# Attention beside two matrix layers on one core: its transfers moved to SyncE's queue, a second k and v buffer, and ScalarE and VectorE in the order of emission through layer 1

## The chip, the cores and the metric

One core of a Trainium2 chip runs the whole program. The time is device microseconds of one execution on that core; the kernel before was run three times. The engines are TensorE (PE, with its weight loads as PEld), VectorE (DVE), ScalarE (ACT), GpSimd (POOL) and SyncE (SP); SP only issues transfers here. Transfers that GpSimd issues show in the profile as queue q0 (software_dynamic), those that SP issues as q1 (hardware_dynamic).

## What is computed

Attention without a softmax, its normalized output laid out as 4608 rows of 512, then two layers without biases. Inputs are float32: q, k, v of 8 batches x 8 heads x 576 positions x 64, and for each layer w_in (512 x 2048) and w_out (2048 x 512).

```python
kv  = np.einsum('bhsd,bhse->bhde', k, v)
out = np.einsum('bhsd,bhde->bhse', q, kv)
x   = out / np.sqrt(np.mean(out * out, axis=-1, keepdims=True) + 1e-06) * g_norm
# x: batch, head, position, 64  ->  4608 x 512
h = x @ w_in;  g = h * (1.0 / (1.0 + np.exp(-1.702 * h)));  x = g @ w_out    # layer 1
h = x @ w_in2; g = h - np.tanh(h);                          y = g @ w_out2   # layer 2
```

## The kernel before, in words

**Stages.** The loop at the end of `body` runs `l` over the two layers and `n` over eight blocks of 576 tokens; block n of layer 1 is batch n of the attention. "Stage n" in this document is stage n of layer 1 (l = 0) unless layer 2 is named. Each stage has two halves. In m1 the block is multiplied by w_in, in m2 by w_out. Every operand is split into two float16 parts, and a product takes three matmuls (lines 631 to 633 in m1, 817 to 819 in m2; lines 845 to 847 and 888 to 890 in the plain forms of stages 0 and 1). From stage 2 on, m1 is a scheme of seven products in place of eight: 54 steps of six matmuls and two more that are run between the first steps of m2. ScalarE copies a bank (L664) and applies the activation (L638), VectorE adds two products (L669). m2 has 28 steps of twelve matmuls; VectorE prepares operands (L692), ScalarE and VectorE split them (L706, L712), five steps ahead of TensorE, and ScalarE and VectorE finish results (L760, L754). The w_out weights of m2 come as 14 streams of 512 KB (`stream`, L733, SP), each for two steps, into four buffers; the first four of a stage are asked for after m1 is emitted, the others when a buffer has been used.

**Work beside the stages.** Three kinds of side work are Python generators that are advanced at the end of every step by `tick`, at a rate per step that the main loop gives (first rate m1, second m2). One advance up to the next `yield` is a "call" in this document.

- `front(b)` computes attention's first part for batch b on TensorE: k-transposed-v products (`head_products`, L425) of units (kt, i), copied by ScalarE (L426), the numerators (`pair_numerators`, L434), their squares and scaled copies on ScalarE (L467, L468), the mean squares (`pair_squares`, L441, read by L443 and L445) and the roots (L507, L508, with two table loads).
- `back(b)` refines the roots on VectorE (`newton`, L513, L514), stores them to `rd` in HBM, loads them back spread over the partitions (L564), multiplies (L571), and splits the result into the float16 operand `xo` of the next stage (`xprep`, L336 on VectorE, L346 on ScalarE, L349 on VectorE).
- `conv1` converts layer 2's weights, 32 items. It loads raw words of item k+1 (`load_words`, L144 and L145, GpSimd), starts item k with ScalarE's L156, goes on with VectorE (L159 to L174), ScalarE's L224 and VectorE's L177, and stores the item (L229 or L232, GpSimd). One item is seven calls; two raw buffers alternate, and the stored item lies in its raw buffer, so the load of item k+1 waits for the store of item k-1. It runs from stage 2's m2 on, from stage 3 at 0.62 and 0.5 calls per step.

In stage n from 2 on, `back(n + 1)` runs beside m1 and, up to stage 5, `front(n + 2)` beside m2. Stage 0 has front(1) and back(1), stage 1 has front(2), back(2) and front(3).

**Transfers of attention.** `part` (L378 to L381) asks for a piece of the packed q, k, v (`atp`), from GpSimd's queue: 1280 words per partition for a unit of k and v (640 KB), 1152 for the q of a pair (576 KB). One region `rk` holds one unit of k and v, so a unit is asked for when the one before has been used; `rq` holds a q, `rs` and `rx` hold results.

**Order.** The tile framework places the instructions of an engine by its own timeline, save inside `tc.manual_schedule`, where the named engines keep the order in which the program emits them. Until the end of stage 1 these are PE, SP, DVE and ACT; from stage 2 on they are PE and SP alone (line 1110). Side instructions get an edge after the latest main instruction of their engine (`issue_after`), so they may come later than emitted, not earlier.

```python
            s[2] += s[1][m]
            while s[2] >= 1:
                s[2] -= 1
```

## Time and profile before

| what | value |
|---|---|
| median of 3 runs | 1529.11 us (1528.98 to 1531.12) |
| profiled execution | 1537.64 us, span 1535.7 us |
| busy share of the span | PE 94%, VectorE 76%, ScalarE 58%, GpSimd 10% |
| layer 1, stages 0 to 7 | 35 to 867 us of the span |
| layer 2 | 867 to 1536 us |
| chain that ended last | PE 45%, DVE 19%, issue 19%, DMA 11%, ACT 5% |

Matmuls overlap in their records, so a busy TensorE is not one at its peak: 288 columns show as some 0.29 us each and start 0.12 us after one another. The rows below give, for a stretch, each engine's busy time with its instructions in brackets, then TensorE's granted clock (1.00 is 2.4 GHz, 0.50 is 1.2 GHz), the DMA engines' busy share and GB/s. A half of a stage is a stretch between the first m1 matmul and the first m2 matmul of a block, or back.

### The profile page before, as it was taken

The page shows a single profiled execution, that of the slowest core. Times are in us where ns is not written, and L with a number is a line of the kernel's source. Part 1 is how long each engine was busy: PE and PEld are TensorE (multiplying, and loading weights), DVE is VectorE, ACT ScalarE, POOL GpSimd, SP SyncE. Part 2 cuts the span into 40 slices and gives each one's busy share as a digit, 9 for nine tenths or more (in the row PEclk, how much of TensorE's full clock was granted, in tenths as well). Part 3 has the DMA queues.
Part 4 walks back from the last instruction along what each step waited for, and adds up shares of the span by engine and source line. Part 5 has one row for each costly group of instructions (what it writes and reads, how often), then busy time and mean ns, then how long its engine had stood idle before and what let it go on. Part 6 is the DMA issues. An engine that isn't in the chain of part 4 may idle for free.

```text
span 1535.7 us, 29954 instructions
## 1 busy us (share of the span) xinstructions
PE 1441.6 (94%) x11922; PEld 1112.7 (72%) x11922; DVE 1159.7 (76%) x2237; ACT 892.7 (58%) x1871; POOL 152.5 (10%) x238
## 2 busy tenths in 40 slices
PE   6999978998899889998999999999999999999999
PEld 5667756676666666766777777777777777777777
DVE  3998878394885976967978686887778787868585
ACT  5775554664765756747656564645565555656463
POOL 0001010102322222111110000000000000000000
PEclk9999999999999999999999999999999999999999
DMA  8776836437477387384586516061523334240504
GB/s 285 220 239 192 249 92 203 129 115 249 125 238 226 90 269 225 124 287 131 178 292 228 181 34 222 14 203 39 171 85 132 124 104 136 71 154 31 194 15 155
DMA packets 104684, 247.55 MB, mean 161 GB/s; under 512 B 10624, under 2 KB 55296, under 8 KB 104544
## 3 DMA queue, kind: packets, MB, share of 16 engines
q1 hardware_dynamic: 83504, 161.49, 32.6%
q0 software_dynamic: 21040, 84.15, 17.4%
q8 instruction: 93, 1.52, 0.4%
q14 instruction: 47, 0.39, 0.1%
HBM read 202.62 MB, written 42.98 MB: 160 GB/s over the span
## 4 chain that ended last, share of the span: by engine, by line
PE 45%; DVE 19%; issue 19%; DMA 11%; ACT 5%; POOL 1%; SPq 0%; DVEq 0%; ACTq 0%; POOLq 0%
PE X L817 4%; PE X L818 4%; PE X L819 4%; PE X L631 3%; PE X L632 3%; PE X L633 3%; DVE gt L692 3%; DVE jt L712 3%; DMA scratch<-rd 2%; PE Y L817 2%; PE Y L819 2%; PE Y L818 2%; PE Z L631 2%; PE Z L633 2%; PE Z L632 2%
## 5 line engine op out<-in xcount | busy, mean ns | idle before, releaser
L706 ACT ACTIVATE jt<-gt 128x576 f16<-128x576 f32 x420 | 284.5, 682 | 179.7 <-PE X L819 73.6
L712 DVE SCALAR_TENSOR_TENSOR jt<-gt,jt 128x576 f16<-128x576 f32 x420 | 312.9, 753 | 95.9 <-ACT jt L706 92.8
L817 PE MATMUL X<-jt,st 128*128 128x288 f16 x960 | 278.6, 290 | 16.8 <-ACT mscratch L760 14.8
L818 PE MATMUL X<-jt,st 128*128 128x288 f16 x960 | 278.4, 290 | 3.7 <-DVE jt L712 3.7
L819 PE MATMUL X<-jt,st 128*128 128x288 f16 x960 | 278.1, 290 | 0.0
L631 PE MATMUL X<-xo,wi 128*128 128x288 f16 x896 | 256.8, 287 | 19.5 <-ACT mscratch L664 17.8
L632 PE MATMUL X<-xo,wi 128*128 128x288 f16 x896 | 256.8, 287 | 0.0
L633 PE MATMUL X<-xo,wi 128*128 128x288 f16 x896 | 256.7, 286 | 0.0
L632 PEld LDWEIGHTS <-wi 128*128 128x128 f16 x1568 | 153.6, 98 | 83.1 <-issue 43.5
L818 PEld LDWEIGHTS <-st 128*128 128x128 f16 x1680 | 165.9, 99 | 60.6 <-issue 18.5
L817 PEld LDWEIGHTS <-st 128*128 128x128 f16 x1680 | 165.8, 99 | 55.8 <-issue 11.6
L819 PEld LDWEIGHTS <-st 128*128 128x128 f16 x1680 | 165.9, 99 | 52.4 <-issue 9.1
L631 PEld LDWEIGHTS <-wi 128*128 128x128 f16 x1568 | 153.7, 98 | 41.1 <-issue 1.8
L633 PEld LDWEIGHTS <-wi 128*128 128x128 f16 x1568 | 153.7, 98 | 39.3
L664 ACT COPY mscratch<-X 128x288 f32<-128x288 f32 x336 | 130.7, 393 | 80.3 <-PE X L633 63.6
L692 DVE TENSOR_TENSOR gt<-gt 128x576 f32<-128x576 f32 x240 | 175.7, 749 | 0.6
L631 PE MATMUL Z<-xo,wi 128*128 128x288 f16 x448 | 128.3, 286 | 16.0 <-DVE mscratch L669 15.6
L818 PE MATMUL Y<-jt,st 128*128 128x288 f16 x480 | 138.1, 288 | 3.3 <-DVE jt L712 3.3
L817 PE MATMUL Y<-jt,st 128*128 128x288 f16 x480 | 138.3, 288 | 0.7 <-DVE mscratch L669 0.5
L819 PE MATMUL Y<-jt,st 128*128 128x288 f16 x480 | 138.3, 288 | 0.0
L669 DVE TENSOR_TENSOR mscratch<-Z,mscratch 128x288 f32<-128x288 f32 x224 | 101.3, 452 | 46.7 <-ACT mscratch L664 23.6
L633 PE MATMUL Z<-xo,wi 128*128 128x288 f16 x448 | 128.4, 287 | 0.0
(240 smaller groups left out, 2482.1 us busy)
## 6 DMA issues: line engine op xcount, KB each, us to landing
st<-wod SPq DMA_DIRECT2D x210, 512.0 KB, 4.8
scratch<-atp POOLq DMA_DIRECT2D x28, 640.0 KB, 6.1
scratch<-x2d SPq DMA_DIRECT2D x32, 288.0 KB, 5.6
cbk<-w_out POOLq DMA_DIRECT2D x32, 256.0 KB, 3.9
cbk<-w_in POOLq DMA_DIRECT2D x32, 256.0 KB, 3.8
scratch<-atp POOLq DMA_DIRECT2D x14, 576.0 KB, 5.5
scratch<-rd POOLq DMA_DIRECT2D x28, 288.0 KB, 6.3
x2d<-mscratch SPq DMA_DIRECT2D x28, 288.0 KB, 5.5
```

The costliest lines, as they stand in the source:

```text
L631: nc.tensor.matmul(out=out, lhsT=wh, rhs=xh, start=fresh and kt == 0, stop=False, skip_group_check=k)
L632: nc.tensor.matmul(out=out, lhsT=wh, rhs=xl, start=False, stop=False, skip_group_check=k)
L633: nc.tensor.matmul(out=out, lhsT=wl, rhs=xh, start=False, stop=kt == 1, skip_group_check=k)
L664: main(nc.scalar.copy(out=b.ap, in_=x))
L669: main(nc.vector.tensor_tensor(out=b.ap, in0=add[0], in1=b.ap, op=ALU.add))
L692: tt = lambda o, a, b: main(nc.vector.tensor_tensor(out=G[:, :, o, :], in0=G[:, :, a, :], in1=G[:, :, b, :], op=ALU.subtract))
L706: main(nc.scalar.activation(out=j[:, :, 0, :], in_=GT[STEPS2[i][1]][:, :, QD[STEPS2[i][0]], :], func=AF.Copy, scale=SX))
L712: main(nc.vector.scalar_tensor_tensor(out=j[:, :, 1, :], in0=GT[STEPS2[i][1]][:, :, QD[STEPS2[i][0]], :], scalar=SX, in1=j[:, :, 0, :], op ...
L817: nc.tensor.matmul(out=out, lhsT=wh, rhs=xh, start=a, stop=False, skip_group_check=k)
L818: nc.tensor.matmul(out=out, lhsT=wh, rhs=xl, start=False, stop=False, skip_group_check=k)
L819: nc.tensor.matmul(out=out, lhsT=wl, rhs=xh, start=False, stop=z, skip_group_check=k)
```

## The change

- `part` issues on SP in place of GpSimd, and so do back's store of the roots and the loads that spread them (they were on GpSimd too).
- k and v of both units of a pair have a buffer: unit 0 in `rk`, unit 1 in `rs`, which grows by 128 columns. `front` runs both head products at once, then one call later the numerators, and asks for the next pair's pieces as their regions come free.
- `back(b)` asks for all three first pieces of batch b+1: the first after the store of the roots, q after the second multiplication, the second k and v buffer as its last act. There are more calls between the store of the roots, the loads and the multiplication (two, four and eight).
- VectorE and ScalarE keep the order of emission in layer 1 from stage 2 on too.
- Rates: stage 0 from 0.55 and 1.0 to 0.8 and 1.7, stage 1 from 0.85 and 0.9 to 1.2 and 1.2, back in m1 from 0.5 to 0.7, front in m2 from 0.75 to 0.8. conv1's rates stay.
- One of two buffers of the start (`kv1`) moves into `rs` until stage 0 is begun.

```diff
-SCRATCH, MAIN = 6472, 7 * 256
+SCRATCH, MAIN = 16 * 288 + 128 + 1280 + 576, 7 * 256
...
-                      ((0, 8 * H), (8 * H, 12 * H), (12 * H, 16 * H), (16 * H, SCRATCH)))
+                      ((0, 8 * H), (8 * H, 12 * H + P), (12 * H + P, 16 * H + P), (16 * H + P, SCRATCH)))
...
-    kvt = [cp.tile([P, P], F32, name=f"kv{i}") for i in range(2)]
+    kvt = [cp.tile([P, P], F32, name="kv"), rs(P)]
+    kvt1, kvt[1] = kvt[1], kvt[1].ap
...
         t = yield from reg.need(n)
-        nc.gpsimd.dma_start(out=t.ap[:, 0:n], in_=atp[b - 1, kt, :, a:a + n])
+        nc.sync.dma_start(out=t.ap, in_=atp[b - 1, kt, :, a:a + n])
         return t
...
-    def unit_kv(b, u):
-        return part(b, u // 2, rk, 2 * T + u % 2 * 1280, 1280)
-
-    def fetch(b):
-
-        ahead[b] = yield from unit_kv(b, 0)
-        ahead[b] = ahead[b], (yield from queries(b, 0))
+    def unit_kv(b, kt, i):
+        return part(b, kt, (rk, rs)[i], 2 * T + i * 1280, 1280)
...
         if b not in ahead:
-            yield from fetch(b)
-            yield
-            yield
-        kb, qb = ahead[b]
+            ahead[b] = []
+            for g in (unit_kv(b, 0, 0), queries(b, 0), unit_kv(b, 0, 1)):
+                ahead[b].append((yield from g))
+            yield
+            yield
+        ka, qb, kb = ahead[b]
         for kt in range(2):
-            for i in range(2):
-                head_products(i, kb.ap[:, 0:1280])
-                kb.free()
-                if (kt, i) != (1, 1):
-                    kb = yield from unit_kv(b, 2 * kt + i + 1)
-                for _ in range(4 if i == 0 else 1):
-                    yield
+            for i, t in ((0, ka), (1, kb)):
+                head_products(i, t.ap)
+                t.free()
+            if kt == 0:
+                ka = yield from unit_kv(b, 1, 0)
+            yield
             xbs[b, kt] = yield from rx.need(4 * H)
...
-                if j == 1:
-                    qb.free()
-                    if kt == 0:
-                        qb = yield from queries(b, 1)
                 yield
                 yield
+            qb.free()
+            if kt == 0:
+                qb = yield from queries(b, 1)
+            yield
             pair_squares(kt, ex.ap)
             ex.free()
             yield
+            if kt == 0:
+                kb = yield from unit_kv(b, 1, 1)
+                for _ in range(5):
+                    yield
...
         y.free()
-        nc.gpsimd.dma_start(out=rd[b], in_=t.ap)
+        yield
+        yield
+        nc.sync.dma_start(out=rd[b], in_=t.ap)
         t.free()
-        yield
+        more = b < NS - 1
+        if more:
+            ahead[b + 1] = [(yield from unit_kv(b + 1, 0, 0))]
+        for _ in range(4):
+            yield
...
-                nc.gpsimd.dma_start(out=t.ap[c * HD:(c + 1) * HD, :].rearrange("p (g n) -> p g n", g=4),
-                                    in_=rows[2 * kt + c].partition_broadcast(HD))
+                nc.sync.dma_start(out=t.ap[c * HD:(c + 1) * HD, :].rearrange("p (g n) -> p g n", g=4),
+                                  in_=rows[2 * kt + c].partition_broadcast(HD))
             rb.append(t)
-        for _ in range(5):
+        for _ in range(8):
             yield
...
             rb[kt].free()
+            if kt and more:
+                ahead[b + 1].append((yield from queries(b + 1, 0)))
             yield
...
-        if b < NS - 1:
-            yield from fetch(b + 1)
+        if more:
+            ahead[b + 1].append((yield from unit_kv(b + 1, 0, 1)))
...
-                    bk = add_side(both(1, xo[1]), 0.55, 1.0)
+                    bk = add_side(both(1, xo[1]), 0.8, 1.7)
                 elif n == 1:
-                    bk = add_side(two(), 0.85, 0.9)
+                    bk = add_side(two(), 1.2, 1.2)
                 elif n < NS - 1:
-                    bk = add_side(back(n + 1, xo[(n + 1) % 2]), 0.5, 1.0)
+                    bk = add_side(back(n + 1, xo[(n + 1) % 2]), 0.7, 1.0)
...
-                man.enter_context(tc.manual_schedule(engines=frozenset([ENG.PE, ENG.SP])))
+                both_too = [] if l else [ENG.DVE, ENG.Activation]
+                man.enter_context(tc.manual_schedule(engines=frozenset([ENG.PE, ENG.SP] + both_too)))
...
-                fr = add_side(front(n + 2), 0.0, 0.75)
+                fr = add_side(front(n + 2), 0.0, 0.8)
```

## Rows read from the trace of the kernel before

**Rows 1.** Busy time by stretch: halves in stages 2, 3, 3, 5, 6, then layer 2.
```profile
272.40:323.50 51.10, 46.35 (x387) 33.74 (x384) 27.67 (x52) 32.79 (x76) 4.65 (x8) 0.93 0.29 91
...
380.70:427.20 46.50, 40.70 (x321) 31.08 (x320) 37.50 (x77) 33.72 (x76) 12.43 (x18) 1.00 0.45 123
427.20:485.80 58.60, 54.07 (x483) 38.73 (x482) 42.27 (x79) 31.87 (x57) 16.07 (x23) 0.94 0.77 246
636.60:691.80 55.20, 53.12 (x485) 38.43 (x483) 40.53 (x76) 30.21 (x55) 10.07 (x16) 0.97 0.80 258
...
738.50:781.10 42.60, 42.60 (x350) 34.02 (x349) 37.57 (x70) 23.97 (x41) 6.48 (x10) 1.00 0.67 214
867.30:907.10 39.80, 39.80 (x326) 31.66 (x324) 30.59 (x67) 24.18 (x61) 0.00 (x0) 1.00 0.18 57
```

**Rows 2.** TensorE's waits, 200 to 800 us: who waited for whom, total, times, longest.
```profile
PE Z L631 <- DVE mscratch L669: 15.6, 12, 3.4
PE X L817 <- ACT mscratch L760: 14.8, 4, 5.3
PE X L631 <- ACT mscratch L664: 13.2, 12, 1.9
PE AT L425 <- DMA scratch<-atp: 3.7, 1, 3.7
```

**Rows 3.** Timeline of ScalarE in stage 3's m2; idle time before in brackets.
```profile
460.57 0.66 ACT L156 ACTIVATE cbk<-cbk 128x512 f32<-128x512 f32 x1 [4.83 <-DMA cbk<-w_out]
```

**Rows 4.** Timeline of GpSimd in the same stretch.
```profile
445.36 1.53 POOL L232 DMA_DIRECT2D wod<-cbk  x2 [3.86 <-DVE cbk L177]
...
453.12 0.71 POOL L144 DMA_DIRECT2D cbk<-w_out  x1 [4.18 <-DMA wod<-cbk]
```

**Rows 5.** Busy time by stretch: stretches at the lower granted clock, two calls.
```profile
149.90:153.30 3.40, 3.40 (x18) 1.97 (x18) 3.20 (x11) 0.98 (x3) 0.00 (x0) 0.50 0.87 233
...
306.90:313.70 6.80, 5.51 (x24) 3.38 (x24) 6.24 (x12) 3.27 (x7) 0.56 (x1) 0.50 0.24 73
...
460.50:467.30 6.80, 5.72 (x25) 3.49 (x25) 4.39 (x10) 2.51 (x5) 1.42 (x2) 0.50 0.48 163
...
sum 20.40, PE 17.91 PEld 11.13 DVE 12.85 ACT 7.44 POOL 4.88; mean PE 4.48 PEld 2.78 DVE 3.21 ACT 1.86 POOL 1.22
```

**Rows 6.** Timeline of ScalarE at the start of stage 3's m1.
```profile
382.19 1.28 ACT L507 ACT_TABLE_LOAD   x1
```

**Rows 7.** Timeline of VectorE in stage 3's m1.
```profile
398.19 1.36 DVE L571 TENSOR_TENSOR scratch<-scratch 128x1152 f32<-128x1152 f32 x1 [2.99 <-DMA scratch<-rd]
```

**Rows 8.** Stage 3: cbk alone (DVE, ACT, POOL); scratch, gt (PE and PEld ahead).
```profile
380.70:427.20 46.50, 11.49 (x23) 4.83 (x6) 8.88 (x12) 1.00 0.45 123
...
380.70:427.20 46.50, 0.00 (x0) 0.00 (x0) 12.34 (x20) 5.82 (x11) 3.56 (x6) 1.00 0.45 123
427.20:485.80 58.60, 7.46 (x128) 3.80 (x128) 0.00 (x0) 5.12 (x8) 2.76 (x5) 0.94 0.77 246
...
380.70:427.20 46.50, 0.00 (x0) 0.00 (x0) 8.98 (x12) 15.04 (x33) 1.00 0.45 123
```

**Rows 9.** A group of VectorE, stage 3's m1: count, busy, mean, idle before.
```profile
L177 DVE TENSOR_TENSOR cbk<-cbk 128x896 f16<-128x896 f32 x3 | 3.3, 1089 | 2.7 <-ACT cbk L224 2.7
```

**Rows 10.** Issues of transfers, stage 3's m1, then m2: count, KB each, us to landing.
```profile
cbk<-w_out POOLq DMA_DIRECT2D x6, 256.0 KB, 3.8
...
st<-wod SPq DMA_DIRECT2D x13, 512.0 KB, 6.4
scratch<-atp POOLq DMA_DIRECT2D x4, 640.0 KB, 7.2
cbk<-w_out POOLq DMA_DIRECT2D x8, 256.0 KB, 4.6
```

**Rows 11.** TensorE's waits, 146 to 152 us.
```profile
PE X L846 <- DVE xo L363: 0.9, 1, 0.9
```

**Rows 12.** Timeline of GpSimd at the start of the program.
```profile
1.33 1.24 POOL L380 DMA_DIRECT2D scratch<-atp  x2 [0.25 <-issue]
```

More of the change, by code (lines that the diff above doesn't have):

```diff
@@ L1016, in body @@
             raise RuntimeError("left")
-    for x in yt:
+    for x in yt + [kvt1]:
         x.free()
```

## The prediction

> **What bounds the kernel now.** I read the busy time by stretch first. A stage of layer 2 costs 39.8 us in its first half (m1), with TensorE busy all of it; this is the floor of a half. In layer 1 the same half takes 46.5 us in stage 3, 40.7 of them TensorE. The second half (m2) takes 42.6 us without attention (stage 6) and 55 to 59 us with it (stages 3 and 5 shown), VectorE at 73% there and ScalarE at 55% [rows 1]. So TensorE is the bound, and layer 1 is longer than its matmuls because TensorE waits. The list of TensorE's waits between 200 and 800 us names for whom: ScalarE's L760 in m2 (14.8 us in four waits, the longest 5.3), VectorE's L669 and ScalarE's L664 in m1 (15.6 and 13.2 us), once a transfer of k and v (3.7 us) [rows 2].
>
> Next, what holds those engines. In stage 3 ScalarE stood 4.83 us at L156, the first operation on a raw layer-2 weight, until its transfer had landed; L760, which TensorE needs, was queued behind it [rows 3]. That transfer had been issued at 453.12 us after GpSimd had waited 4.18 us for the write-out that it had issued at 445.36 us from the same buffer [rows 4]. After such a stall the granted clock is 0.50, the lower level (1.2 GHz): four stretches of 20.4 us together in the m2 halves of stages 2 to 5, and one each in stage 1's start (3.4 us) and in stage 2's m1 (6.8 us); they cost half their length [rows 5].
>
> In m1 the first holds are ScalarE's table loads for the roots, 1.28 us each, two of them, at 382 us when m1 has begun [rows 6], and VectorE's L571, the scaling by the roots, which waited 2.99 us for the spread roots to land, everything of VectorE behind it [rows 7].
>
> **The change part by part.** I count positions in calls of the side generators: a step of m1 is 39.8/54 = 0.737 us at the floor.
>
> *A, m2 of stages 2 to 5.* Emission order puts L156 of weight item k+1 nine calls after item k-1 is finished; at m2's rate of 0.5 that is 18 steps, over 18 x 1.47 us = 26 us, against 15 us from that write-out's issue to L156's start [rows 3, 4]. Before, the order was free, and it had moved items out of m1: 23 instructions (three items) on cbk in m1, where the rate of 0.62 emits 33/7 = 4.7 [rows 8]. GpSimd now has only these transfers, so the k/v wait of 3.7 us goes too. What can go: 14.8 + 3.7 [rows 2] + half of 20.4 [rows 5] = 28.7 us. I take 22, leaving over a microsecond per half for waits that a fixed order makes. Bounds: 29 and 4.
>
> *B, m1 of stages 3 to 6.* Three effects. The front now has 20 calls at 0.8, so the roots are emitted at m2's step 25 of 28 and the table loads leave m1. The spread roots are loaded at call 7 and used at call 15, eight calls at 0.7, 8.4 us; the kernel before has five at 0.5, 7.4 us; the store goes at call 3, and SP has nothing else in m1, so L571's wait should go. Against this VectorE has more to do in m1: 1.7 more weight items at 11.49/2.9 = 4.0 us of VectorE (the 23 instructions are 2.9 items of eight), +6.8, and of the twelve operations on gt (8.98 us) only five are emitted here, -5.2; the back's 12.34 us stay [rows 8]. That makes 37.5 + 1.6 = 39.1 us [rows 1], and the 2.7 us in which VectorE waited for ScalarE's copy of a weight item stay [rows 9]: 41.8 us, against 46.5. The back's scaling and splitting now fall into 22 steps (22 to 43) in place of 30, so VectorE is denser there; I take a third of the 4.7, 1.5 per stage, -6 for four. Bounds: -20 (near the floor) and +34 (third rival).
>
> *C, m1 of stage 2.* No weight items are emitted here and VectorE is half idle (27.67 of 51.1 us [rows 1]); L571 held TensorE and then the clock for 6.8 us [rows 5]. 3.4 of clock and some 3 of wait can go; I take -5, bounds -7 and 0.
>
> *D, start of stage 1.* The side work of stage 0 did not fit: 35 calls against 33 ticks, so the x operands came late (0.9 us, once [rows 11]) and the clock fell for 3.4 us [rows 5]. Now 42 calls against 52 ticks. I take -3, bounds -4 and 0.
>
> *E, the rest of stage 1.* ScalarE, VectorE and SP were in emission order here before as well. The back's work comes earlier, but front(3) follows back(2) in the same call that issues its second k/v transfer, so TensorE must wait for it (7.2 us of landing [rows 10]). I take 0 between -10 and +8.
>
> *F, stage 0.* The first k/v and q transfers were issued at 1.33 us [rows 12]. Now all three stand on SP behind layer 1's weights, two calls (two steps of 1.47 us) ahead of their use, and a k/v transfer takes 7.2 us [rows 10]. TensorE waits perhaps 4 us, partly given back as the weight conversion goes on meanwhile. I take +3, bounds 0 and +8.
>
> *G, the weight streams of m2 on SP.* Streams 0 to 3 of a stage were issued as the preceding m2 ended. Now the back's transfers stand ahead of them on SP, and the last, the second k/v buffer for the next batch, is emitted at step 45 of 54 and waits until VectorE has done with that region. Behind it stand the four streams. Cover: 9 steps, 6.6 us; a stream takes 6.4 us and the k/v transfer 7.2 us [rows 10], the two overlapping. I take 1.5 us late per stage in stages 2 to 5, +6, bounds 0 and +14.
> By the Trainium skill ("DMA: Bandwidth & Descriptors", section "Queues, rings and completion order") a DMA engine takes turns between queues but works through one queue in its order, so attention's bytes, which took turns with the streams from GpSimd's queue, would now go wholly ahead of them; by that rule G is at its upper bound and the sum 8 us higher. No stage of the trace has both on SP.
>
> Attention's matmuls stay (128 per batch, 7.46 us in stage 3's m2 [rows 8]). The buffer for unit 1 itself costs 128 columns and no instruction.
>
> **Sum:** -22 - 6 - 5 - 3 + 0 + 3 + 6 = -27 us. The profiled execution took 1537.6 us with a span of 1535.7, 8.5 us above the median of 1529.1; taken off the median this gives 1502 us.
>
> **The rivals.**
> 1. *More comes off:* m1 falls within 2 us of its floor, since table loads and the roots' wait were what TensorE felt there: B is -18, and F and G are hidden. 1502 - 12 - 9 = 1481. For it: the first waits of m1 stem from just these. Against: VectorE's 39 us of work leave no room in a half of 40.
> 2. *The weight transfers still land late.* They stay on GpSimd, and if it is their landing and not their place that counts, L156 keeps its waits and A is only -4: 1502 + 18 = 1520. For it: landing follows the DMA load, which is 0.77 in m2 [rows 1], and does not fall. Against: 26 us of lead.
> The Trainium skill ("SBUF — State Buffer", section "SBUF: two separate sides") says that transfers issued from GpSimd starve while VectorE runs certain two-port operations; by that rule these transfers would be late as before. The trace speaks against it: the issues took 0.71 us with VectorE busy around them [rows 4].
> 3. *Slower: L156 waits in m1.* Emission order puts more items there (4.7 for three), and at 0.62 the nine calls between an item's end and the L156 after the next are 14.5 steps, 10.7 us, not 26. If write-out and load need the 15 us that they took in m2 [rows 3, 4], ScalarE stands 4.3 us at every second item, and L664 behind it, which TensorE needs two steps later. Price: 4.7/2 x 4.3 = 10 us per m1, in four stages: B is +34 instead of -6 (part of today's waits hides in it), the sum 1542. The point from which it decides the sign: when B exceeds +21, that is about 3 us late at every second item. For it: early in m1 the spread roots (four transfers) and the next k/v are under way at once. Against: in m1 these loads landed in 3.8 us, not 4.6 [rows 10], with a DMA share of 0.45, not 0.77 [rows 1].
> 4. *Nothing much:* waits go from one queue to the next, 1529.
>
> **How the numbers follow.** About 0.2% (3 us) is what a measurement can tell. Forecast 0.50, rival 1 0.15, rival 2 0.12, rival 3 0.20, rival 4 0.03. For 8 in 10 the range reaches below to rival 1's time, 1480 (half of that case beyond it), and above past rival 2 and the measured 1529 to the middle between 1520 and rival 3's 1542, about 1533; the bounds of E, F and G (+8, +5, +8 beyond the values taken) lie inside it. Faster: all of the first two, most of rival 2, 0.75; within 0.2%: 0.06; slower: 0.19.
>
> **What would show each step.** A: no wait of TensorE above 2 us for L760 in m2 of stages 2 to 5, granted clock 1.00 there, ScalarE's L156 with no wait for a transfer; m2 near 51 to 53 us. B: no table load in the first 10 us of m1; L571 not waiting for a transfer; m1 at 44 to 46 us, VectorE busy about 39 us of it. C and D: clock 1.00 from stage 2's m1 and at stage 1's start. F and E: TensorE's L425 waiting for k/v transfers in stages 0 and 1. G: the first m2 matmuls of stages 2 to 5 waiting 1 to 3 us for a stream. Wrong it would be if L156 still waits for transfers, in m2 or now in m1, with TensorE waiting for L664 behind it.

## The result and the profile after

The changed kernel is slower: 1544.42 us (median of 4 runs, 1543.40 to 1548.96) against 1529.27 (4 runs, 1528.98 to 1531.12), a ratio of 1.0099 with a 95% interval of 1.0084 to 1.0114, or 15 us. The forecast was 27 us faster, and its range ended at 1533. The profiled execution took 1548.96 us with a span of 1547.2, so against the profiled one of before the span grew by 11.5 us. Layer 2 takes the same time (666 and 668 us); all of the loss lies in layer 1.

The table sums halves of layer 1. A half ends here with the last m2 matmul of a stage (m2) or with its first one (m1); stages 0 and 1 stand whole, stage 0 from the start of the span. All runs of the study are in it, and the sections below name its columns.

| kernel | stage 0 | stage 1 | m1 of 2 | m2 of 2 to 5 | m1 of 3 to 6 | m2 of 6 and stage 7 | layer 1 ends |
|---|---|---|---|---|---|---|---|
| before | 146.4 | 125.5 | 51.6 | 231.1 | 183.9 | 129.0 | 867.4 |
| after | 155.5 | 141.0 | 40.1 | 207.1 | 205.3 | 131.7 | 880.8 |
| e1_free | 151.9 | 140.4 | 40.3 | 222.6 | 185.2 | 125.5 | 865.9 |
| e2_before_order | 145.9 | 126.1 | 57.8 | 207.1 | 206.2 | 130.3 | 873.5 |
| e3_rates | 150.6 | 139.9 | 40.1 | 212.6 | 181.9 | 134.6 | 859.7 |
| e4_gap | 153.2 | 131.2 | 41.6 | 207.1 | 207.7 | 131.7 | 872.5 |
| f3_heads | 149.7 | 140.5 | 40.1 | 203.1 | 211.1 | 130.2 | 874.7 |
| f2_rate0 | 151.2 | 142.9 | 40.1 | 207.1 | 209.4 | 130.2 | 880.9 |
| f4_pool_all | 157.4 | 137.0 | 40.1 | 207.1 | 198.8 | 130.2 | 870.6 |
| f1_three | 149.2 | 132.6 | 41.6 | 204.5 | 185.8 | 131.0 | 844.8 |
| g1_order_rates | 146.0 | 128.7 | 58.9 | 212.4 | 195.0 | 134.4 | 875.4 |
| g2_three_lead | 147.2 | 135.4 | 41.8 | 204.5 | 186.4 | 131.2 | 846.5 |
| g3_three_pool | 152.3 | 128.8 | 41.6 | 204.5 | 188.2 | 130.9 | 846.3 |
| h1_stage1_pool | 147.8 | 128.9 | 41.6 | 204.5 | 185.9 | 130.9 | 839.6 |

So the m2 halves gave 24.0 us and stage 2's m1 11.5, as hoped; the m1 halves of stages 3 to 6 took back 21.4, stage 1 took 15.5, stage 0 took 9.1 and the end of the layer 2.7. Each row is one execution. Kernels with the same program in a column show how far a cell can be trusted: stage 0 of the kernel after, e1, e3 and e4 lies between 150.6 and 155.5, m1 of stages 3 to 6 of the kernel after, e4 and f2 between 205.3 and 209.4, stage 1 of the kernel after, e1 and e3 between 139.9 and 141.0.

The kernel after, busy time by stretch: m1 of stage 2, m1 and m2 of stage 3, m2 of stage 5, m2 of stage 6, then layer 2's first m1. These answer to [rows 1].

```profile
296.60:336.70 40.10, 39.15 (x319) 31.12 (x319) 24.80 (x47) 26.35 (x66) 0.00 (x0) 1.00 0.40 124
387.90:441.50 53.60, 42.69 (x326) 32.17 (x324) 40.64 (x82) 32.06 (x74) 13.44 (x18) 0.97 0.54 160
441.50:493.40 51.90, 50.63 (x480) 37.24 (x478) 41.32 (x75) 32.15 (x59) 7.78 (x11) 1.00 0.69 233
643.70:696.20 52.50, 50.80 (x480) 37.24 (x478) 40.39 (x73) 31.00 (x57) 5.42 (x8) 1.00 0.68 228
749.10:797.50 48.40, 44.77 (x351) 34.78 (x350) 39.90 (x72) 21.64 (x39) 5.21 (x8) 0.96 0.56 179
880.80:920.50 39.70, 39.70 (x325) 31.54 (x324) 30.48 (x67) 24.05 (x61) 0.00 (x0) 1.00 0.17 54
```

Stage 2's m1, which has no weight items, runs at layer 2's floor: 40.1 us against 39.7. Stage 3's m1, which has them, takes 53.6, with VectorE busy for 40.64 of them. Both m2 halves have TensorE busy almost throughout at a granted clock of 1.00.

Now for whom TensorE waits in the kernel after, 200 to 800 us, the list that answers to [rows 2]: total, times, longest.

```profile
PE X L640 <- ACT mscratch L673: 29.7, 29, 4.9
PE AT L421 <- DMA scratch<-atp: 9.2, 1, 9.2
PE Z L640 <- DVE mscratch L678: 8.1, 11, 1.2
...
PE X L826 <- ACT mscratch L769: 3.0, 2, 2.5
...
PE Z L826 <- DMA st<-wod: 2.4, 1, 2.4
```

Lines have moved: L673 is the old L664, L678 the old L669, L769 the old L760, L421 the old L425, L157 the old L156. The m2 wait for L760 fell from 14.8 us in four waits to 3.0 in two. The m1 wait for ScalarE's copy of a bank rose from 13.2 us in 12 waits to 29.7 in 29; the one for VectorE fell from 15.6 to 8.1. And there is a single new wait of 9.2 us for k and v, in stage 1.

What ScalarE does in stage 3's m1, where the longest of the 29 waits is: its timeline in the kernel after, with idle time before an instruction in brackets.

```profile
399.11 0.41 ACT L647 ACTIVATE gt<-X 128x288 f32<-128x288 f32 x1
405.21 0.66 ACT L157 ACTIVATE cbk<-cbk 128x512 f32<-128x512 f32 x1 [5.70 <-DMA cbk<-w_out]
405.78 0.39 ACT L673 COPY mscratch<-X 128x288 f32<-128x288 f32 x1
```

This is the third rival's picture: L157 stands until its transfer has landed, and the copy of a bank that TensorE waits for is queued behind it. Over stages 3 to 6 it is five waits, 14.2 us of ScalarE, the one of 5.7 us the largest. TensorE's two longest waits, 4.9 and 3.9 us, stand behind two of them; here is the second, in stage 6, ScalarE and then TensorE:

```profile
723.05 0.66 ACT L157 ACTIVATE cbk<-cbk 128x512 f32<-128x512 f32 x1 [2.81 <-DMA cbk<-w_in]
...
725.49 0.28 PE L640 MATMUL X<-xo,wi 128*128 128x288 f16 x1 [3.94 <-ACT mscratch L673]
```

Of TensorE's other 27 waits for that copy none is longer than 2.1 us, and most come where no L157 waits. The weight items alone in the same half, VectorE's, ScalarE's and GpSimd's instructions on cbk, against the first line of [rows 8]:

```profile
387.90:441.50 53.60, 18.39 (x36) 7.99 (x10) 13.44 (x18) 0.97 0.54 160
```

36 instructions are 4.5 items of eight, where the free order of before had run 23.

The wait of 9.2 us in stage 1 in three lines of the timeline of the kernel after: VectorE, SP, TensorE.

```profile
257.09 0.45 DVE L350 SCALAR_TENSOR_TENSOR xo<-scratch,xo 128x288 f16<-128x288 f32 x1
...
257.56 0.81 SPq L381 DMA_DIRECT2D scratch<-atp  x2
...
262.00 1.33 PE L421 MATMUL AT<-scratch 128*64 128x64 f32 x20 [9.23 <-DMA scratch<-atp]
```

The last instruction of back(2) on VectorE (L350) releases region `rs` at 257.54; only then can SP issue the second k and v, and TensorE, which has reached the head product of front(3) in the same call, stands from 252.8 until they are there at 262.0: 4.8 us until the region is free and 4.4 us of landing. The clock follows it down, as the busy times of the stretch show:

```profile
255.60:265.80 10.20, 3.80 (x31) 2.82 (x32) 5.37 (x9) 0.80 (x2) 0.00 (x0) 0.50 0.37 129
```

### The profile page after: what moved, and what is told of

It reads as the page before. It is cut to its first block, busy times and chain, and to the rows that moved or that the text cites. A ratio compares the mean times of both kernels' runs of the same rounds, so it can differ in the third digit from the quotient of the medians.

```text
span 1547.2 us, 30040 instructions
## 1 busy us (share of the span) xinstructions
PE 1447.3 (94%) x11922; PEld 1115.3 (72%) x11922; DVE 1169.1 (76%) x2237; ACT 885.5 (57%) x1871; POOL 109.5 (7%) x161
## 4 chain that ended last, share of the span: by engine, by line
PE 47%; issue 26%; DVE 15%; DMA 5%; ACT 5%; POOL 1%; SPq 0%; DVEq 0%; ACTq 0%; POOLq 0%
PE X L826 5%; PE X L828 4%; PE X L827 4%; PE X L640 3%; PE X L642 3%; PE X L641 3%; PE Y L826 2%; PE Y L828 2%; PE Y L827 2%; DVE jt L721 2%; PE Z L640 2%; PE Z L642 2%; PE Z L641 2%; DMA cbk<-w_out 1%; DVE gt L701 1%
## 5 line engine op out<-in xcount | busy, mean ns | idle before, releaser
L715 ACT ACTIVATE jt<-gt 128x576 f16<-128x576 f32 x420 | 278.4, 680 | 141.5 <-DVE gt L701 51.4
L826 PE MATMUL X<-jt,st 128*128 128x288 f16 x960 | 275.8, 287 | 4.7 <-ACT mscratch L769 3.0
L827 PE MATMUL X<-jt,st 128*128 128x288 f16 x960 | 275.5, 287 | 0.7 <-DVE jt L721 0.7
L828 PE MATMUL X<-jt,st 128*128 128x288 f16 x960 | 275.4, 287 | 0.0
L673 ACT COPY mscratch<-X 128x288 f32<-128x288 f32 x336 | 131.2, 393 | 83.7 <-PE X L642 68.7
L678 DVE TENSOR_TENSOR mscratch<-Z,mscratch 128x288 f32<-128x288 f32 x224 | 101.7, 454 | 83.5 <-PE Z L642 47.5
```

Of the source, the lines that this page charges most:

```text
L673: main(nc.scalar.copy(out=b.ap, in_=x))
L678: main(nc.vector.tensor_tensor(out=b.ap, in0=add[0], in1=b.ap, op=ALU.add))
L715: main(nc.scalar.activation(out=j[:, :, 0, :], in_=GT[STEPS2[i][1]][:, :, QD[STEPS2[i][0]], :], func=AF.Copy, scale=SX))
L826: nc.tensor.matmul(out=out, lhsT=wh, rhs=xh, start=a, stop=False, skip_group_check=k)
L827: nc.tensor.matmul(out=out, lhsT=wh, rhs=xl, start=False, stop=False, skip_group_check=k)
L828: nc.tensor.matmul(out=out, lhsT=wl, rhs=xh, start=False, stop=z, skip_group_check=k)
```

## The experiments

Theory 1: keeping ScalarE and VectorE in the order of emission is what shortens m2 and lengthens m1, since it holds in m1 the weight items that the free order had moved out of it. Theory 2: the transfers' move to SP's queue does it. Each kernel was compared with runs of before on its own chip (their medians lay between 1530.8 and 1534.3), so the ratios are what is to be compared.

**e1_free**: the kernel after without the order.

```diff
-                both_too = [] if l else [ENG.DVE, ENG.Activation]
+                both_too = []
```

> The changed kernel with VectorE and ScalarE left in the framework's order from stage 2 on; queues, buffers, calls and rates stay changed. Theory 1 (the fixed order makes m1 of stages 3 to 6 long, 49.4 to 53.8 us, because 4.7 weight items run there, and the same order keeps m2 of stages 2 to 5 short, 51 to 52.4): m1 returns to 45 to 47.5 us, m2 goes back up to 54 to 59; in sum 1535 to 1550 us. Theory 2 (m2 is short because GpSimd's queue is rid of attention's transfers, m1 is long because they share SP and the DMA engines at m1's start): m2 stays at 51 to 53, m1 stays at 49 or more; 1540 to 1548 us. Stages 0 and 1 as in the changed kernel by both.

Measured: 1532.71 us, ratio 0.9997 (0.9975 to 1.0019). m1 of stages 3 to 6 goes back to 185.2 (before 183.9), m2 of stages 2 to 5 up to 222.6. One by one the m1 halves are more uneven than expected (50.6, 46.8, 45.6 and 42.1), and the whole is 2 us below its expected range. Two TensorE waits of this kernel, 300 to 700 us:

```profile
PE Y L826 <- DMA st<-wod: 9.9, 3, 4.0
PE X L826 <- ACT mscratch L769: 8.4, 3, 4.2
```

The order made both shifts. And all the rest of the change together was worth nothing when the order was free. The first line is step G: with a free order the second k and v buffer is released late in m1, the four streams stand behind it on SP, and m2 of stages 3, 4 and 5 starts 3 to 4 us late. With the order fixed this wait is gone.

**e2_before_order**: the kernel before with the order, and nothing else of the change.

```diff
-                man.enter_context(tc.manual_schedule(engines=frozenset([ENG.PE, ENG.SP])))
+                man.enter_context(tc.manual_schedule(engines=frozenset([ENG.PE, ENG.SP] + ([] if l else [ENG.DVE, ENG.Activation]))))
```

> The kernel before with one part of the change: VectorE and ScalarE in the order of emission from stage 2 to 7. Theory 1: m1 of stages 3 to 6 rises from 45 to 47 to 49 to 54 us, m2 of stages 3 to 5 falls from 55 to 59 to 51 to 54; in sum 1520 to 1535 us, since stages 0 and 1 stay. Theory 2: m2 stays at 55 or more as the transfers still share GpSimd's queue, and m1 stays near 46: 1526 to 1535 us with the halves as before. The stages tell, not the sum.

Measured: 1546.23 us, ratio 1.0087 (1.0053 to 1.0121). The sums are those of the kernel after, 207.1 and 206.2 us, with every attention transfer still on GpSimd: theory 2 is out for both. The whole misses the expected 1520 to 1535 us, since the m1 halves took back 22.3 of the 24.0 us and stage 2's m1 grew by 6.2. The list of TensorE's waits of this kernel, 200 to 800 us, has

```profile
PE X L631 <- ACT mscratch L664: 34.6, 35, 5.2
PE Z L631 <- DVE mscratch L669: 10.3, 13, 2.1
```

and its ScalarE never waits for a weight transfer at L156 between 300 and 800 us. So the order lengthens the m1 halves as much without a single wait of the third rival's kind, with 35 or 36 instructions on cbk in each. These halves hold waits that the kernel after does not have, for the late roots (g1 below), so this run does not tell how much the landing of the words is worth in the kernel after.

**e3_rates**: the kernel after with fewer weight items in m1 and more in m2.

```diff
-                rate(later, 0.62, 0.5)
+                rate(later, 0.45, 0.8)
```

> The changed kernel with the weight items' rate from stage 3 on 0.45 in m1 and 0.8 in m2 in place of 0.62 and 0.5 (3.5 items in m1 in place of 4.8, 3.2 in m2 in place of 2). Theory 1: each item costs m1 some 2 to 2.5 us there (9 to 13 us over the 40.1 of stage 2's m1, which has none, for 4.7 items) and little in m2: m1 of stages 3 to 6 falls by 2 to 4 us each, m2 rises by 0 to 1.5; 1530 to 1540 us. Rival (m1 is held by the transfers that stand at its start, not by the number of items): m1 falls by less than 1 us, 1542 to 1547 us.

Measured: 1531.61 us, ratio 0.9999 (0.9978 to 1.0019), and m1 of stages 3 to 6 at 181.9 us, 23.4 less. Stage 3's m1 and m2 in this kernel, and below them the weight items alone in the m1:

```profile
381.90:426.80 44.90, 40.98 (x324) 31.45 (x323) 35.77 (x72) 31.21 (x73) 9.65 (x13) 1.00 0.59 172
...
426.80:478.00 51.20, 50.58 (x480) 37.36 (x478) 45.27 (x83) 32.42 (x59) 11.17 (x16) 1.00 0.74 251
...
381.90:426.80 44.90, 12.69 (x25) 6.46 (x8) 9.65 (x13) 1.00 0.59 172
```

Eleven instructions on cbk less (5.7 us of VectorE) shorten this m1 by 8.7 us, of which part is L157's wait, 1.3 us here against 5.7; the other three fall by 4.0, 4.1 and 6.9, all more than or at the top of what was expected. Stage 3's m2, which takes the items, is no longer for it, but over stages 2 to 5 the m2 halves grow by 5.5 us. One line of the main loop gives back 13 of the 15 us by the medians and all of it by the ratios.

**e4_gap**: six empty calls between back(2) and front(3) in `two`, and stage 1's m2 rate from 1.2 to 1.4 so that the work still fits.

```diff
         yield from both(2, xo[0])
+        for _ in range(6):
+            yield
         yield from front(3)
...
-                    bk = add_side(two(), 1.2, 1.2)
+                    bk = add_side(two(), 1.2, 1.4)
```

> The changed kernel with six empty calls between back(2) and front(3) in stage 1, and rate 1.4 in place of 1.2 in its m2 so that all calls still fit. Theory 3 (stage 1 is 15 us longer because TensorE stands 9.45 us at the head products for a k/v transfer asked for in the same call, and then runs at the lower clock): the wait falls under 4 us and stage 1 is shorter by 7 to 12 us, 1532 to 1538 us. Rival (VectorE bounds that m2, and the wait only falls where VectorE is behind anyway): shorter by less than 3 us, 1541 to 1546 us.

Measured: 1545.47 us, ratio 1.0080 (1.0058 to 1.0103). Stage 1 falls from 141.0 to 131.2, and the wait for k and v with it:

```profile
PE AT L421 <- DMA scratch<-atp: 2.6, 1, 2.6
```

Stage 1 does what the theory says, and its cause is shown. The time of the whole lies in the rival's range (1541 to 1546): the intervals of this kernel and of the kernel after overlap, so the runs as a whole do not show the gain.

**f3_heads**: both head products ahead of both copies of k and v.

```diff
-        nc.scalar.copy(out=kvp[:, i], in_=AT[i][:, 384:448])
...
+            for i in range(2):
+                nc.scalar.copy(out=kvp[:, i], in_=AT[i][:, 384:448])
```

> The kernel after, with both head products ahead of both copies of k and v (as it is, the second head product waits for ScalarE's copy of the first: 3.1 us once in stage 0 and twice 0.53 us per second half). Theory: that wait is a loss of its own, new with the two buffers: the 3.1 us of stage 0 go, and about 1 us of each second half of stages 1 to 5, in sum 3 to 8 us less than the kernel after's 1544. Rival: the other waits of those calls (for transfers, for the banks' readers) take the place of it: less than 2 us.

Measured: 1543.50 us, ratio 1.0067 (1.0042 to 1.0092): by the ratios some 5 us less than the kernel after (0.0032 of 1530), as expected, though the two intervals overlap. TensorE's waits for ScalarE's copies, 30 to 800 us, after and then here:

```profile
PE AT L421 <- ACT kv L422: 6.3, 11, 3.1
```
```profile
PE AT L429 <- ACT kv L456: 1.1, 1, 1.1
```

m2 of stages 2 to 5 falls from 207.1 to 203.1, 1 us each as expected. The sum of the m1 halves is 5.8 us longer, of which 4 is what executions of the same program differ by there.

**f2_rate0**: stage 0's side work at 1.1 calls per step of m2 in place of 1.7.

```diff
-                    bk = add_side(both(1, xo[1]), 0.8, 1.7)
+                    bk = add_side(both(1, xo[1]), 0.8, 1.1)
```

> The kernel after, with the side work of stage 0 at 0.8 and 1.1 calls per step in place of 0.8 and 1.7, which still fits (43 ticks for 42 calls). Theory that the rate of 1.7 crowds VectorE and ScalarE in stage 0's second half: it falls from 58 us to 53 to 55 us, the whole by 3 to 5 us. Rival, that attention's transfers standing among layer 1's weights on SyncE's queue make that half longer: unchanged within 1 us.

Measured: 1551.35 us, ratio 1.0123 (1.0100 to 1.0147), not clearly slower than the kernel after, as the intervals overlap. Stage 0's m2 fell by only 2 us (58.1 to 56.2), less than the theory and more than the rival said; e3, whose stage 0 is that of the kernel after, has 56.3 there, so not even these 2 us need be the rate's. At L421 at the start of stage 1's m1 TensorE stood 4.1 us, for nothing that the profile shows. The theory that the rate crowds stage 0 is refuted.

**f4_pool_all**: all attention transfers on GpSimd again, the order and both buffers kept (the same edit at `part`, back's store and back's loads).

```diff
-        nc.sync.dma_start(out=t.ap, in_=atp[b - 1, kt, :, a:a + n])
+        nc.gpsimd.dma_start(out=t.ap, in_=atp[b - 1, kt, :, a:a + n])
```

> The kernel after, with all of attention's transfers issued by GpSimd again, the order of ScalarE and VectorE and both buffers kept. If it is the order that cuts the second halves of stages 2 to 5, they stay at 51 to 53 us and the first halves of stages 3 to 6 stay at 49 to 54; if the queue does it, the second halves go back above 54. What SyncE's queue costs stages 0 and 1 shows there: by the theory that k and v come late in stage 1 because front(3) follows in the same call, stage 1 stays at 139 to 142 us; by the rival, that they stand behind the streams on SyncE's queue, it falls below 135. The whole: 1540 to 1548 by the first, 1532 to 1538 by the second.

Measured: 1544.78 us, ratio 1.0079 (1.0054 to 1.0103). m2 stays at 207.1, so the queue has no part in it. Stage 1 falls to 137.0, between the two expectations. What the queue does touch is ScalarE's wait for the weights, 300 to 800 us, after and then here:

```profile
ACT cbk L157 <- DMA cbk<-w_out: 8.0, 2, 5.7
ACT cbk L157 <- DMA cbk<-w_in: 6.2, 3, 2.8
```
```profile
ACT cbk L157 <- DMA cbk<-w_out: 5.1, 5, 1.8
ACT cbk L157 <- DMA cbk<-w_in: 2.1, 2, 1.4
```

With half of that wait gone (14.2 to 7.2 us), m1 of stages 3 to 6 is 6.5 us shorter, nearly all of it in stages 3 and 6: that much of the 21 us goes with the third rival's mechanism, and the move to SP's queue brought it on. Stage 6 shows the rest: its m1 has no such wait here, and takes 49.5 us where it took 46.6 before.

**f1_three**: the three repairs together, those of e4 and f3 and these rates. The second edit raises the weight items' rate in stage 2's m2; the expectation speaks of stage 7.

```diff
-                rate(later, 0.62, 0.5)
+                rate(later, 0.45, 0.75)
...
-                add_side(later, 0.0, 0.85)
+                add_side(later, 0.0, 1.0)
```

> The kernel after with three repairs at once: both head products ahead of both copies; six empty calls between back(2) and front(3) in stage 1, with 1.4 calls per step in its second half; and from stage 2 on 0.45 and 0.75 calls per step, with the weight items that are left over at one call per step in stage 7. If the three losses are separate, the sum is 1544 - 14 (rates) - 5 (gap) - 5 (heads) = 1520 us, between 1515 and 1526, ahead of both kernels. If they are one loss that only moves along the queues, it comes out near the kernel with the rates alone, 1529 to 1533.

Measured: 1517.85 us, ratio 0.9899 (0.9854 to 0.9943): faster than before and after. By the ratios the gains over the kernel after were 15 us (e3), 3 (e4) and 5 (f3), together 23; here they are 31, with some 7 us of uncertainty. So the losses are separate, and their gains add up at least.

**g1_order_rates**: the kernel before with the order and e3's rates, without the second buffer, the new front and SP's queue.

```diff
-                rate(later, 0.62, 0.5)
+                rate(later, 0.45, 0.8)
```

> The kernel before with the order of ScalarE and VectorE in layer 1 alone (as the second run of the first call) and, from stage 3 on, 0.45 and 0.8 calls of the weight items per step. If the order and its rates are all that the change is worth, it comes out near 1531 or below (1546 - 15), with first halves of stages 3 to 6 at 44 to 47 us and second halves of stages 2 to 5 at 51 to 56, as in the kernel after with these rates. If the second k/v buffer and SyncE's queue carry a part that the crowding had hidden, it stays above 1537.

Measured: 1541.87 us, ratio 1.0068 (1.0044 to 1.0091), so the second of its two cases holds in time. Its m1 of stages 2 and 3:

```profile
274.80:333.70 58.90, 47.19 (x391) 34.44 (x392) 25.44 (x48) 33.32 (x78) 4.66 (x8) 0.86 0.26 80
385.00:432.90 47.90, 41.14 (x319) 31.45 (x317) 35.54 (x72) 34.44 (x78) 13.18 (x19) 0.96 0.46 129
```

Against e3, with the same order and rates, m1 of stage 2 is 18.8 us longer and m1 of stages 3 to 6 are 13.1 longer. Stage 2's m1 still has half of front(3) in it. In stage 3, with VectorE as busy as in e3 (35.54 and 35.77 us), the roots come late: ScalarE's first table load of m1 and VectorE's waits at L571, 300 to 700 us, in this kernel:

```profile
386.30 1.28 ACT L507 ACT_TABLE_LOAD   x1
...
DVE scratch L571 <- DMA scratch<-rd: 8.6, 4, 4.4
```

In e3 the loads stand at 372.81 and 378.87 us, ahead of m1, and L571's successor waits for no transfer. So the order needs the new front: alone it gives 1.0087, and 1.0068 with the rates set again, but 0.9999 with the rates and the rest of the change. SP's queue, which the expectation names too, is not what helps: f4 has m1 of stage 2 at 40.1 with all of attention on GpSimd. Whether the rest needs the order is not shown: in the free order it gives 0.9997 (e1), and no run has the three repairs in the free order.

**g2_three_lead**: f1 with eight calls of lead for the second k and v in stages 0 and 1 in place of five.

```diff
-                for _ in range(5):
+                for _ in range(8 if b < 4 else 5):
...
-                    bk = add_side(two(), 1.2, 1.4)
+                    bk = add_side(two(), 1.2, 1.6)
```

> The kernel with the three repairs, where TensorE still waited twice in stage 1 for a k/v transfer asked five calls ahead (2.6 and 2.8 us), with eight calls of lead in stages 0 and 1 in place of five, and 1.6 calls per step in stage 1's second half so that the work still fits. Theory that the lead in calls is what k and v lack in stage 1: both waits fall below 0.7 us and the time by 3 to 6 us, to 1512 to 1515 at the first batch's rate of before. Rival, that the work packed closer behind them takes it back: within 2 us of the kernel with the three repairs, or above it.

Measured: 1517.91 us, ratio 0.9905 (0.9874 to 0.9935), no gain over f1: stage 0's m2 falls from 57.8 to 52.9 us, and stage 1 takes 2.8 us more. TensorE's wait for k and v in stage 1, 147 to 283 us, in f1 and then here:

```profile
PE AT L421 <- DMA scratch<-atp: 5.0, 2, 2.6
```
```profile
PE AT L421 <- DMA scratch<-atp: 4.7, 2, 2.6
```

Lead in calls was not what was missing.

**g3_three_pool**: f1 with f4's edit.

> The kernel with the three repairs and all of attention's transfers issued by GpSimd again. In the kernel after itself this took ScalarE's longest wait for a weight in a first half from 5.7 to 1.8 us and the ratio from 1.0099 to 1.0079. If SyncE's queue gains nothing here either, the ratio is 0.985 to 0.990, the same as the kernel with the three repairs or a little below. If the move to SyncE is what makes room once the crowding is gone, it is 0.992 or more.

Measured: 1520.35 us, ratio 0.9929 (0.9905 to 0.9952). The number lies on the side of the second expectation, but its interval overlaps that of f1 and the profiled spans agree (1514.3 and 1514.0 us): what the queue is worth over the whole can't be told. In stage 1 it can: that is 3.8 us shorter here, and h1 repeats it. Stage 0 is 3.1 longer and m1 of stages 3 to 6 are 2.4 longer, no more than executions of the same program differ by.

**h1_stage1_pool**: f1, where only stage 1's k, v and q go through GpSimd.

```diff
-        nc.sync.dma_start(out=t.ap, in_=atp[b - 1, kt, :, a:a + n])
+        e = nc.gpsimd if b in (2, 3) else nc.sync
+        e.dma_start(out=t.ap, in_=atp[b - 1, kt, :, a:a + n])
```

> The kernel with the three repairs, where the k/v and q transfers of stage 1 alone (batches 2 and 3) are issued by GpSimd, all others by SyncE. Eight calls of lead left TensorE's waits of 2 to 3 us for k and v in stage 1 where they were; with all of attention on GpSimd the first of them was gone and stage 1's first half 4 us shorter, but first halves of stages 3 to 5 were 1 us longer each. Theory that in stage 1 k and v stand behind SyncE's streams of the weight sums: the first half of stage 1 is 60 to 62 us in place of 65, and the ratio 0.984 to 0.989. Rival, that the sums are due in any case and TensorE waits for them next: stage 1 in all stays at 131 to 134 us, ratio 0.990 or more.

Measured: 1512.18 us (6 runs, 1507.35 to 1516.02), ratio 0.9861 (0.9835 to 0.9887), as the first theory has it: stage 1's m1 is 61.0 us in place of 65.3. Why, the timelines of the issuing engines show. SP in f1, then GpSimd here:

```profile
159.20 0.81 SPq L266 DMA_DIRECT2D wod<-cbk  x1
163.68 0.36 SPq L284 DMA_DIRECT2D cbk<-wod  x1
164.13 0.46 SPq L266 DMA_DIRECT2D wod<-cbk  x1
164.68 1.00 SPq L381 DMA_DIRECT2D scratch<-atp  x2
```
```profile
156.87 0.55 POOL L382 DMA_DIRECT2D scratch<-atp  x1 [5.96 <-PE AT L430]
160.79 0.53 POOL L382 DMA_DIRECT2D scratch<-atp  x1 [3.37 <-ACT ms L439]
```

In f1 both transfers go out together at 164.68 us, behind a load of the weight sums (L284, at 163.68), for which SP had waited until the store of the line above had landed; from GpSimd the same two go out at 156.87 and 160.79, each as soon as its buffer is free. This kernel has the lowest ratio of the study, 1.4% under before; its interval overlaps that of f1.

## Why the prediction was wrong

**A was right.** m2 of stages 2 to 5 fell by 24.0 us, forecast 22. No L157 waits for a transfer there, the clock is 1.00, TensorE's waits for L760's successor are down to 0.6 us (the other 2.5 us of the list are in stage 6), and the halves lie at 51 to 53 us as named. The second rival (the transfers still land late in m2) did not come about: the lead of 18 steps was enough, although in stage 3's m2 these loads now took 5.9 us to land, against 4.6 [rows 10]. By the rule cited there ("SBUF — State Buffer" of the Trainium skill) they would have been late as before; no run here shows that, and e2, with all of attention on GpSimd too, has no L156 waiting for one.

**B is the step that failed.** It said -6, "m1 at 44 to 46 us, VectorE busy about 39 us of it"; it is +21.4, with halves of 49 to 54. Its quantities were right: 4.5 items in stage 3's m1 (forecast 4.7), 18.39 us of VectorE on them (4.7 x 4.0 = 18.8), 40.64 us of VectorE in all (39.1), L571's successor without a wait for a transfer. What was wrong is the way from work to time: to VectorE's sum the step added 2.7 us for the time in which VectorE itself waits, and took 41.8 as what the half would need. Already before, VectorE stood idle for 9.0 us of that half [rows 1]; after, it is 13.0, and 46.5 over stages 3 to 6. Nor is it the amount of work. e1 has nearly the same VectorE work in these four halves (157.0 us against 158.8) and, in the free order, takes 185.2 us where the kernel after takes 205.3, with VectorE idle for 28.2. Stage 4's m1 in the kernel after, then in e1:

```profile
493.30:542.70 49.40, 41.45 (x327) 31.62 (x325) 38.60 (x80) 31.12 (x73) 13.15 (x18) 1.00 0.62 173
...
492.60:539.40 46.80, 40.60 (x325) 31.42 (x323) 39.77 (x82) 32.45 (x76) 8.93 (x12) 0.99 0.53 156
```

What differs is what stands ahead of what. In m1 TensorE needs an answer of ScalarE and VectorE within a step or two, and in the order of emission each weight item emitted in between is put ahead of that answer. From e3 to the kernel after VectorE's work in the four halves grows by 15.5 us and the halves by 23.4, the waits at L157 included; to f4, with half of these waits, it is 15.3 and 16.9. The free order of before had shown this, in the 23 instructions of [rows 8]: three items were all that it put into m1, and the step read that row only as a number of instructions. e3 shows what was needed: 25 instructions again, by the rate, and the half takes 44.9.

The third rival gave the right sign and nearly the right time (1542), the time in part by luck: it had B at +34 where 21.4 was measured, and nothing for stages 0 and 1 together (D, E and F), which took 24.6. B did cross the +21 that it named. Its mechanism, L156 waiting for its transfer, is real but the smaller part: f4, with half of these waits gone, is 6.5 us shorter there, and e2 has m1 halves as long without one.

No step had a term for stage 6's m2, which grew from 42.7 to 48.4 us: TensorE waits 2.5 us there for L769, which stands behind L225 of a weight item, and the granted clock falls to 0.50 for 3.4 us. In the free order of e1 it takes 42.8.

**C was better than forecast.** Stage 2's m1 fell by 11.5 us, forecast 5. Of this, 3.8 are attention's matmuls that before ran in stage 2 and after run in stage 1. The remaining 8 put it on the floor. It is neither the order (e1 has 40.3 without it) nor the queue (f4 has 40.1): g1, with the order and without the rest, has 58.9, so it is the new front with its buffer and back's calls and rates, which no run takes apart.

**D was right and E wrong.** The clock no longer falls as stage 1 starts (its first fall is at 180.5 us), but D and E together were forecast at -3, and stage 1 took 15.5 us more, 12 of them not just moved from stage 2. The step did say that front(3) follows back(2) in the same call and that TensorE must wait for the second k and v, but set that off against back's earlier work. What it missed is when the transfer can be issued at all: `rs` is in use until VectorE's last L350, 4.8 us after TensorE is ready, and the landing (4.4 us, not 7.2) begins only there, with no matmul beside it. With the stalls the granted clock was 0.50 for 23.9 us of stage 1, against 6.8 before. e4 shows 9.8 us of it, h1 another 4 in m1.

**F went past its upper bound, and not by its mechanism.** Stage 0 took 9.1 us more, forecast 3 with 8 as the bound; in e1, e3 and e4, with the same stage 0, it is 4.2 to 6.8. No k or v transfer makes TensorE wait there. In m1, 3.1 us are a wait that the prediction did not see, the second head product behind ScalarE's copy of the first (f3). m2 is 5.4 us longer, and the traces show where it begins. The two table loads of the roots, which step B moved out of the later m1 halves, now stand at the seam of stage 0's halves, ahead of four activations (L868) that TensorE needs; no step had a term for that. ScalarE, then TensorE, in the kernel after:

```profile
95.34 1.28 ACT L508 ACT_TABLE_LOAD   x1
...
97.57 1.28 ACT L483 ACT_TABLE_LOAD   x1
...
102.87 0.40 ACT L868 ACTIVATE gt<-Y 128x288 f32<-128x288 f32 x1
...
103.32 0.40 PE L897 MATMUL Y<-jt,st 128*128 128x288 f16 x1 [2.44 <-ACT gt L868]
```

TensorE waits 3.4 us there in two waits, against 0.3 before, and the granted clock fell to 0.50 for 6.8 us at 102.0 and for 3.4 at 125.9; before it did not fall in that half. Every kernel with the calls of the change in stage 0 has these waits, whatever the queue (f4) and the rate of m2 (f2), and 56 to 59 us in this half. g2 alone, with three more calls, has the loads behind the last of these activations:

```profile
95.60 0.40 ACT L869 ACTIVATE gt<-Z 128x288 f32<-128x288 f32 x1
...
96.60 1.28 ACT L509 ACT_TABLE_LOAD   x1
```

There TensorE does not wait for them, and the half takes 52.9 us, as before (52.7). No run was made to test this by itself.

**G did not cost in stages 2 to 5.** The rule of the Trainium skill ("DMA: Bandwidth & Descriptors", section "Queues, rings and completion order") would have had the streams late there; the trace of after has no such wait in these stages, and one of 2.4 us in stage 1. e1 has it, three waits of 9.9 us together. In e1 the first of the four streams goes out 2.4 us before TensorE is ready for stage 3's m2 (at 429.07 and 431.4 us), in the kernel after 6.1 us before (435.40 and 441.5). So what counts is how long ahead of m2 the second k and v can be issued, which the order had moved ahead.

## What to carry to other kernels

When an engine is put into a fixed order, the rates at which side work is emitted become the schedule: set them again, half by half, for the work that the free order had chosen to place there. Count not whether an engine's work fits into a stretch but how much of it stands ahead of each answer that the critical engine waits for. And a transfer can start no earlier than its buffer is released and its issuing engine has come to it in program order; more lead in the program helps with neither.

## What the runs showed of the hardware that was not expected

- A transfer's issuing engine mattered by its place in that engine's program. The four k, v and q transfers of stage 1's m1, moved from SP to GpSimd, took 4.3 us off it (65.3 to 61.0 us; 60.9 in g3), because SP stood at a load whose data were not ready. The Trainium skill ("DMA: Bandwidth & Descriptors", section "Issuing engines are not separate DMA queues") says that issuing from several engines saves only the time to initiate a transfer; here the measurement differs, as it also saves what the issuing engine waits.
- The lower clock outlasts the stall that it follows. TensorE stood from 252.8 to 262.0 us, the granted clock was 0.50 from 255.6 to 265.8, and TensorE busy 3.80 of these 10.2 us: the first 3.8 us of work after the wait ran at 1.2 GHz.
- Taking attention off GpSimd's queue did not make the transfers that stayed there faster: ScalarE's waits at L157 were 14.2 us in all with attention on SP and 7.2 with it on GpSimd.
